# A tail rebuilt: last gh2 among the LayerNorm-backward rows, column sums by ones matmuls, the last modulation gradients on PE, two groups of products moved to GpSimd

## The chip, the cores and the metric

One core of one Trainium2 chip. The metric is the device time of one execution in microseconds (us), the median of several. On one core most runs of a kernel agree within 0.3%; every run quoted here is undisturbed. Engines are named as in the profile: PE (TensorE matmul), DVE (VectorE), ACT (ScalarE), POOL (GpSimd), SP (the queue that issues most DMAs).

## The reference

Forward and backward pass of a block with two LayerNorms, modulated by `c`: a spectral filter (rfft2, times a complex weight, irfft2) and a gated bilinear layer. Sequence 2048, width 576, hidden width 4608, bf16. Outputs: the forward result and the gradients of eight inputs.

```python
mod = (silu(c) @ w_mod).reshape(1, 6, 1, 576)          # sa, ca, ga, sb, cb, gb
h = layernorm(x) * (1 + ca) + sa
x = x + ga * irfft2(rfft2(h) * (w_r + 1j * w_i))       # spectral filter
h = layernorm(x) * (1 + cb) + sb
x = x + gb * (((h @ w_gate) * (h @ w_up)) @ w_down)    # gated bilinear
# ... vjp of all this for grad_out
```

## The kernel before

The change touches the last quarter of the kernel, after the last gate/up block. I cut that tail into four stages by events on PE: (1) the last gh2 (gradient that reaches the second LayerNorm) and its 16 LayerNorm-backward rows, with weight gradients as filler, up to the first inverse-stage matmul; (2) eight spectral units up to the first matmul of the final rows; (3) sixteen final rows up to the last column sum; (4) the end. "Filler" is a list of independent matmul blocks that the program deals out between dependent steps, so that PE has something to do. A list scheduler then orders the instructions of each engine by dependences and its own estimate of times; each engine runs its list in that order.

The complex multiply of a unit, and the loop of the units:

```python
def multiply(X, W, P1, P2, Y, SD, conj, u):
    tt(P1[:], X[:], W[:], MUL)                         # L457   tt = DVE tensor_tensor
    tt(P2[:], X[:], W[:, :, ::-1, :], MUL)             # L458
    tt(Y[:, 0], P1[:, :, 0, :], P1[:, :, 1, :], ADD)   # L459
    tt(Y[:, 1], P2[:, :, 1, :], P2[:, :, 0, :], SUB)   # L461
    if u:
        tt(SD[:, 0:2], Y[:, :, 0, :], Y[:, :, 1, :], ADD)   # L465
        tt(SD[:, 2:4], Y[:, :, 0, :], Y[:, :, 1, :], SUB)   # L466

load_X(0)                                              # ahead of the units
load_X(1)

def grad_W(u, gY):                                     # gradient of the spectral weights
    gw = gw_r.next()
    tt(Q[:], Xls[u][:], gY[:], MUL)                    # L1068
    tt(gw[:, :, 0, :], Q[:, :, 0, :], Q[:, :, 1, :], ADD)
    tt(Q[:], Xls[u][:], gY[:, :, ::-1, :], MUL)
    tt(gw[:, :, 1, :], Q[:, :, 0, :], Q[:, :, 1, :], SUB)
    # ... stores
for s in range(9):
    # ... stage_b of unit s (PE, ACT, DVE), filler
    if s:
        u = s - 1
        X = X_r.next()
        stage_c(u, Zs[u], X, RS)                       # PE L441, copy by ACT L442
        multiply(X, Ws[u], P1, P2, Y_t, SD_t, True, u)
        fill.run(4.0)
        stage_ci(u, Y_t, SD_t, Gt)                     # PE L492, needs the multiply
        gws[u] = grad_W(u, X)
        # ... loads of W and X for unit u + 2
```

The column sums of a row, and one final row:

```python
def diag_sums(a, b, j, b0, b1, c1, col):               # ten small matmuls
    for m, (d0, n) in enumerate(CH):
        mm(bank[0:n, b1, col + m:col + m + 1], a[:, d0:d0 + n], ones[:, 0:1], ...)
        # ... and a[:, block].T @ b[:, block], of which only the diagonal is used

ts(n[:], n[:], rstd1[:, jj:jj + 1], nmr1[:, jj:jj + 1], MUL, ADD)   # DVE
ln_bwd(gh, n, mod[:, SCA, :], ...)
fill.run(2.5)
diag_sums(gh, n, jj, 6, 7, 0, 64)
fill.run(2.5)
```

## Time and profile before

| stage, us (profiled run) | (1) | (2) | (3) | end | span |
|---|---|---|---|---|---|
| before | 113.3 | 106.1 | 109.8 | 34.4 | 1569.0 |

The median is 1572.26 us (1569.24 to 1573.04, 4 runs). The first matmul of the final rows is at 1424.8; the prediction put it at about 1428, so its second stage is 3.3 us longer and its third shorter.

```profile
PE bank L492 <- DVE arena L465: 3.7, 5, 1.4
```

### The profile page before, as it was taken

The page shows a single profiled execution, that of the slowest core. Times are in us where ns is not written, and L with a number is a line of the kernel's source. Part 1 is how long each engine was busy: PE and PEld are TensorE (multiplying, and loading weights), DVE is VectorE, ACT ScalarE, POOL GpSimd, SP SyncE. Part 2 cuts the span into 40 slices and gives each one's busy share as a digit, 9 for nine tenths or more (in the row PEclk, how much of TensorE's full clock was granted, in tenths as well). Part 3 has the DMA queues.
Part 4 walks back from the last instruction along what each step waited for, and adds up shares of the span by engine and source line. Part 5 has one row for each costly group of instructions (what it writes and reads, how often), then busy time and mean ns, then how long its engine had stood idle before and what let it go on. Part 6 is the DMA issues. An engine that isn't in the chain of part 4 may idle for free. (4 is left out here: it accounts for less than half of the span.)

```text
span 1569.0 us, 28400 instructions
## 1 busy us (share of the span) xinstructions
PE 1479.0 (94%) x11245; PEld 989.8 (63%) x11268; DVE 811.0 (52%) x1800; ACT 515.6 (33%) x1017; POOL 261.1 (17%) x380
## 2 busy tenths in 40 slices
PE   7799997999999999999999999999999888999991
PEld 4344442677677668667767766866776666676771
DVE  6424496633543453353354345335337765778865
ACT  5656665212212221221221122122123344344331
POOL 1122321212202202211220220221110110000000
PEclk9899999999999999999999999999999999999995
DMA  9655886977558557646755854765663597567941
GB/s 277 193 145 158 205 232 157 196 152 169 123 106 184 128 109 153 150 120 127 168 128 101 184 128 108 155 145 123 128 156 100 163 258 226 157 182 206 267 123 49
DMA packets 440998, 248.76 MB, mean 159 GB/s; under 512 B 318048, under 2 KB 418336, under 8 KB 440352
## 3 DMA queue, kind: packets, MB, share of 16 engines
q1 hardware_dynamic: 418256, 177.19, 50.4%
q0 software_dynamic: 22464, 69.62, 14.5%
q8 instruction: 88, 1.44, 0.4%
q14 instruction: 46, 0.38, 0.1%
q10 hardware_dynamic: 144, 0.13, 0.0%
HBM read 96.90 MB, written 74.20 MB: 109 GB/s over the span
## 5 line engine op out<-in xcount | busy, mean ns | idle before, releaser
L852 DVE TENSOR_TENSOR arena<-arena,bank 128x576 f32<-128x576 f32 x272 | 204.9, 754 | 305.1 <-PE bank L846 305.1
L740 ACT CAST arena<-bank 128x512 bf16<-128x512 f32 x144 | 84.4, 586 | 390.4 <-PE bank L730 373.4
L846 PE MATMUL bank<-arena 128*128 128x288 bf16 x576 | 164.6, 286 | 0.0
L843 PE MATMUL bank<-arena 128*128 128x288 bf16 x576 | 163.9, 285 | 0.5 <-DVE arena L850 0.2
L845 PE MATMUL bank<-arena 128*128 128x288 bf16 x576 | 164.3, 285 | 0.0
L844 PE MATMUL bank<-arena 128*128 128x288 bf16 x576 | 164.1, 285 | 0.0
L785 PE MATMUL bank<-arena 128*128 128x256 bf16 x1152 | 150.3, 274 | 7.9 <-ACT arena L790 5.4
L1032 PE MATMUL bank<-arena 128*128 128x288 bf16 x1152 | 152.9, 288 | 0.0
L765 PE MATMUL bank<-arena 128*128 128x288 bf16 x1152 | 147.9, 289 | 4.5 <-DVE arena L773 4.5
L734 PE MATMUL bank<-arena 128*128 128x512 bf16 x576 | 149.6, 382 | 1.5 <-DMA arena<-arena 1.5
L789 PE MATMUL bank<-arena 128*128 128x256 bf16 x1152 | 150.6, 274 | 0.0
L736 PE MATMUL bank<-arena 128*128 128x512 bf16 x576 | 148.7, 381 | 0.0
L765 PEld LDWEIGHTS <-arena 128*128 128x128 bf16 x1152 | 113.2, 99 | 37.4 <-issue 4.7
L1032 PEld LDWEIGHTS <-arena 128*128 128x128 bf16 x1152 | 111.0, 98 | 32.0 <-issue 3.2
L785 PEld LDWEIGHTS <-arena 128*128 128x128 bf16 x1152 | 111.3, 98 | 24.8 <-issue 11.4
L789 PEld LDWEIGHTS <-arena 128*128 128x128 bf16 x1152 | 112.5, 98 | 13.9
L744 DVE TENSOR_TENSOR arena<-arena 128x512 bf16<-128x512 bf16 x144 | 61.2, 425 | 107.1 <-ACT arena L740 107.1
L790 ACT CAST arena<-bank 128x256 bf16<-128x256 f32 x144 | 53.5, 372 | 184.9 <-PE bank L789 184.9
L734 PEld LDWEIGHTS <-arena 128*128 128x128 bf16 x576 | 50.4, 98 | 80.6 <-issue 31.6
L736 PEld LDWEIGHTS <-arena 128*128 128x128 bf16 x576 | 56.6, 98 | 68.6 <-issue 1.1
L741 ACT CAST arena<-bank 128x512 bf16<-128x512 f32 x144 | 84.8, 589 | 24.7 <-PE bank L736 23.3
L321 ACT CAST arena<-bank 128x1024 bf16<-128x1024 f32 x72 | 72.8, 1011 | 55.3 <-PE bank L317 27.9
(217 smaller groups left out, 2206.3 us busy)
## 6 DMA issues: line engine op xcount, KB each, us to landing
ghh_d<-arena POOLq DMA_DIRECT2D x72, 256.0 KB, 3.6
arena<-ghh_d POOLq DMA_DIRECT2D x36, 512.0 KB, 5.4
hh_d<-arena SPq DMA_DIRECT2D x36, 512.0 KB, 4.5
arena<-hh_d SPq DMA_DIRECT2D x16, 1152.0 KB, 7.7
out_dram<-arena POOLq DMA_DIRECT2D x36, 256.0 KB, 5.1
arena<-in_B_w_down_dram POOLq DMA_DIRECT2D x18, 288.0 KB, 4.1
out_dram<-arena POOLq DMA_DIRECT2D x36, 144.0 KB, 5.6
arena<-in_B_w_down_dram SPq DMA_DIRECT2D x4, 1296.0 KB, 8.4
```

The costliest lines, as they stand in the source:

```text
L734: mm(bank[:, bg, :], w[:, m, fs], h2T[:, js, m, :], odd == 0 and m == 0, odd == 1 and m == 3)
L736: mm(bank[:, bu, :], w[:, 4 + k, fs], h2T[:, js, m, :], odd == 0 and k == 0, odd == 1 and k == 3)
L741: ac.copy(u[:], bank[:, bu, :])
L765: mm(bank[:, b0 + h, 0:288], sf[:, 0, fb, j, :], go[:, j, 288 * h:288 * h + 288], j == 0, j == 15)
L785: mm(bank[:, st["b"], 0:256], h2p[:, j, 128 * m:128 * m + 128], sf[:, 1 + w, :, j, :], j == 0, False)
L789: mm(bank[:, st["b"], 0:256], h2p[:, j, 128 * m:128 * m + 128], sf[:, 1 + w, :, j, :], False, j == 15)
L843: mm(o, xT[:, 1, 0, cs], wT[p][:, 0, 0, hs], True, False)
L844: mm(o, xT[:, 2, 0, cs], wT[p][:, 0, 1, hs], False, False)
L845: mm(o, xT[:, 1, 1, cs], wT[p][:, 1, 0, hs], False, False)
L846: mm(o, xT[:, 2, 1, cs], wT[p][:, 1, 1, hs], False, True)
L852: tt(dst, dst, src, ADD)
L1032: mm(bank[:, yb, 0:288], hl[:, fb % 18, 128 * (j % 2):128 * (j % 2) + 128], wdr[:, fb, 288 * h:288 * h + 288], fb == 0, fb == 35)
```

## The change

Its intent: less PE work in the rows (column sums of whole rows by a matmul with ones on column groups, instead of diagonal blocks), less DVE work in the rows and the units (normalisation to ACT, three row products and the gradient of the spectral weights to POOL), gh2 spread among the rows instead of ahead of them, and no serial gradient work at the end: four of the six modulation gradients go into the units, the last two are made by small matmuls with a transposed `w_mod`. Buffers move with it, so the loads of X now start only after the last weight gradients. The core of the diff:

```diff
+        def column_sums(srcs, b, j, w):
+            for h in range(2):
+                for i, a in enumerate(srcs):
+                    mm(bank[w * i:w * i + w, b + h, 0:288], ones[:, 0:w], a[:, 288 * h:288 * h + 288], j == 0, j == 15, ...)
@@ rows of stage 1
-            ts(n[:], n[:], rstd2[:, j:j + 1], nmr2[:, j:j + 1], MUL, ADD)
+            act(n[:], n[:], ACT.Identity, bias=nmr2[:, j:j + 1], scale=rstd2[:, j:j + 1])
-            tt(gn[:], gx[:], mod[:, SGA, :], MUL)
-            fold(Fj.unsqueeze(1), gn.unsqueeze(1), 1)
-            diag_sums(b, n, j, 2, 3, 0, 192)
-            diag_sums(gx, yl[j], j, 5, 3, 64, None)
+            po.tensor_tensor(gs[:, 0:288], gx[:, 0:288], mod[:, SGA, 0:288], MUL)
+            po.tensor_tensor(gs[:, 288:576], gx[:, 575:287:-1], mod[:, SGA, 575:287:-1], MUL)
+            po.tensor_tensor(pg[:], gx[:], yl[j][:], MUL)
+            column_sums([acc_b(j), q, pg], 2, j, 32)      # two rows later
@@ spectral units
-        load_X(0)
-        load_X(1)
-            tt(Q[:], Xls[u][:], gY[:], MUL)
+            gt = po.tensor_tensor
+            gt(Q[:], Xls[u][:], gY[:], MUL)
             # ... the other three alike
+                if s == 1:
+                    fill.flush()                          # the last weight gradients
+                    fill = yfill
+                    load_X(0)
+                    load_X(1)
                 stage_ci(u, Y_t, SD_t, Gt)
                 gws[u] = grad_W(u, X)
+                if mgs:
+                    mod_grad(*mgs.pop(0))                 # six groups, one per unit
@@ final rows and end (cut)
-                ts(n[:], n[:], rstd1[:, jj:jj + 1], nmr1[:, jj:jj + 1], MUL, ADD)
+                act(n[:], n[:], ACT.Identity, bias=nmr1[:, jj:jj + 1], scale=rstd1[:, jj:jj + 1])
-                diag_sums(gh, n, jj, 6, 7, 0, 64)
+                column_sums([gh, q], 6, jj, 64)
+            if j == 2:
+                sp.dma_start_transpose(out=wmT[:], in_=w_mod[:, 0:2 * D])
+                # fold of the early modulation gradients: 4 small matmuls into bank 0, 2 DVE copies
-        mod_grad(SCA, mod[:, SCA, :])
-        mod_grad(SSA, mod[:, SSA, :])
+        # ... ten one-row matmuls, nine scaled rows, 45 one-column matmuls with wmT
```

## The prediction

> **What bounds the kernel now.** I read the page's parts 1 and 2 first: PE is busy 94% of the span, so the 366 us after the last gate/up block (1203 us on) is the only place with room. Then I cut the tail, from the end of the last gate/up matmuls (1205.2, from PE's timeline), at the first inverse-stage matmul (1318.6), the first of the final rows (about 1428) and the last column sum (1534.7), and asked for the busy time of each engine in each stretch. Columns: window, length, then busy us (and count) of PE, PEld, DVE, ACT, POOL, then granted clock, DMA share, GB/s.
>
> ```profile
> 1205.20:1318.60 113.40, 97.49 (x921) 75.64 (x920) 82.08 (x211) 52.32 (x127) 13.63 (x20) 0.94 0.84 227
> 1318.60:1428.00 109.40, 102.72 (x817) 73.82 (x817) 73.62 (x114) 40.79 (x95) 0.00 (x0) 0.97 0.62 169
> 1428.00:1534.70 106.70, 104.67 (x921) 79.28 (x919) 83.12 (x236) 43.06 (x110) 0.00 (x0) 1.00 0.68 193
> 1534.70:1569.00 34.30, 1.63 (x6) 0.40 (x4) 16.44 (x53) 2.48 (x8) 0.00 (x0) 0.54 0.17 49
> ```
>
> The reader should see four different stages. The first (last gh2, LayerNorm-backward rows with the last weight gradients as filler) leaves PE idle for 16 us; the second (eight spectral units) and third (sixteen final rows) are PE-bound through the filler, the y products; the last has almost no PE and 34 us of serial work. Its length is mostly one store. In the DMA view (out<-in, queue, count, KB each, us to landing) that is the last line, issued at 1552.5 and landing 15.2 us later:
>
> ```profile
> out_dram<-arena SPq DMA_DIRECT2D x1, 1.1 KB, 15.2
> ```
>
> The chain of waits of a spectral unit, from the timeline, is the next thing to keep in mind: PE's unit matmuls (L441), ACT's copy (L442), DVE's complex multiply (L457 to L466) and back to PE (L492), with four filler blocks of nine matmuls (L1032) laid over it.
>
> ```profile
> 1354.44 1.15 PE L441 MATMUL bank<-arena 128*128 128x290 bf16 x8
> 1355.18 1.21 ACT L442 ACTIVATE arena<-bank 128x580 bf16<-128x580 f32 x2
> 1356.41 0.76 DVE L457 TENSOR_TENSOR arena<-arena 128x1160 bf16<-128x1160 bf16 x1 [3.54 <-ACT arena L442]
> ...
> 1358.51 1.36 DVE L1068 TENSOR_TENSOR arena<-arena 128x1160 f32<-128x1160 bf16 x1
> 1359.79 0.45 DVE L465 TENSOR_TENSOR arena<-arena 128x580 bf16<-128x580 bf16 x1
> 1360.16 0.45 DVE L466 TENSOR_TENSOR arena<-arena 128x580 bf16<-128x580 bf16 x1
> 1360.30 0.28 PE L492 MATMUL bank<-arena 128*128 128x256 bf16 x1 [1.40 <-DVE arena L465]
> ```
>
> X is ready at 1356.4 and PE goes on at 1360.3: 3.9 us, just about hidden by the filler. Units follow every 12.7 us. L1068 to L1071 are the gradient of the spectral weights, 1.36 + 0.76 + 1.37 + 0.76 = 4.2 us of DVE per unit.
>
> **What the Trainium skill says.** (1) "SBUF — State Buffer", section "Who interferes with whom": a DVE instruction with two SBUF inputs contends with a GpSimd instruction that reads SBUF; whoever starts first holds the shared port for the whole instruction. The trace agrees. Of 36 POOL additions two met such a DVE instruction, and both times it took 1.7 us where its median is 0.45:
>
> ```profile
> 1235.91 1.41 POOL L774 TENSOR_TENSOR arena<-arena 128x576 f32<-128x576 f32 x1
> 1235.96 1.69 DVE L906 TENSOR_TENSOR arena<-arena 128x576 bf16<-128x576 bf16 x1
> ```
>
> ```profile
> 1285.68 1.42 POOL L774 TENSOR_TENSOR arena<-arena 128x576 f32<-128x576 f32 x1
> 1285.74 1.68 DVE L908 TENSOR_TENSOR arena<-arena 128x576 bf16<-128x576 bf16 x1
> ```
>
> A third POOL addition (1156.42) overlapped a DVE instruction with one PSUM input; that took its usual 0.76. (2) "GPSIMD Engine Reference", section "Elementwise — side-by-side cycle accounting": about 2.6 cycles per element for a two-input operation. The trace gives 1413 ns for 576 columns; with some 0.2 us fixed (an estimate) that is 2.1 ns per column, so 0.8 us for 288, 2.6 for 1160, 1.4 for 580. (3) "TensorE: Matmul & The Clock Gate", section "Part 3: Packing small matmuls": matmuls on different column groups run concurrently. The trace agrees: the two 32-column matmuls L947 and L948 start at the same time, 1230.72.
>
> **The change, part by part.**
>
> First stage. Removed on PE: per row 15 diagonal-sum matmuls (1.07 us from first start to the next block, 1228.34 to 1229.41) and 6 of stage a (0.48 us), 16 rows: 24.8 us. Added: per row six 288-column sums on three column groups, two packs of 0.13, four matmuls of 256 columns (0.11 each) and half of eight packed 128-column ones (0.12): 0.82 us, 13 us in all. Some 9 us of filler is kept for the next stage. PE work falls from 97.5 to about 75 us, and gh2 (16.4 us, so far ahead of the rows) now lies among them. DVE loses per row the normalisation (0.43), one scale (0.36), the SGA product (0.45) and the fold (0.60); it gains split gh2 additions. ACT gets more: per row two scale-and-bias passes at 0.87 (L668's form), two accumulating passes at 0.88, two evacuations at 0.38 and a remainder: 4.5 us, 72 us for sixteen, 78 with the gradients' evacuations. So ACT, not PE, is the floor. With first and last row's latency 85 us instead of 113: -28. POOL gets 0.8 + 0.8 + 1.4 = 3.0 us per row.
>
> Second stage. The y filler starts one unit later (51 us of credit here instead of 62) but 9 us of gradients replace it: about -2.5. At the start the W loads stand behind two loads of 1.2 MB and the modulation weights; I allow 3.5 us of waiting. grad_W leaves DVE for POOL (2 x 2.6 + 2 x 1.4 = 8.0 us per unit), and the early modulation gradients enter DVE (18 pairs of 0.75 + 0.08 + 0.28: 20 us over eight units). If POOL disturbs nobody: +1 in all.
>
> Third stage. Ten sum matmuls per row (0.65) become two packs (0.26): 16 x 0.39 = -6.2; slightly more y filler (80 instead of 78 us): +1.7. Together -4.5. DVE loses the 30 us of modulation gradients, but it is not the bound.
>
> End. 15 us of modulation gradients on DVE go; in their place: copy 0.6, filler 4.4, ten small matmuls 0.8, copies 0.5, filler 4.4, 45 one-column matmuls some 3, four small DVE operations 0.6, issue 0.4, and again a store of 576 two-byte elements, 15.2: 30 us instead of 34.3, with 10 us of filler inside (already counted above as moved): -4.3.
>
> Sum without any disturbance: -28 + 1 - 4.5 - 4.3 = -36, so 1572 - 36 = 1536 us.
>
> **The rivals.** (a) The port lock. The new grad_W needs X and its load, so POOL becomes ready at the moment at which DVE's multiply does. Both then want the port, and the trace shows POOL getting in between two DVE instructions that stand back to back (L936 and L908 at 1285.7). If each of POOL's four operations comes between two of the six of DVE, the multiply takes 2.9 + about 7.5 = 10.4 us instead of 3.9, PE waits 6.5 us in every unit that is so hit, seven of eight: +45. In the rows the same lock costs DVE up to 2.5 us of each row; with DVE's own 3.6 us and ACT's 4.5 I take 5.8 us per row, so the first stage needs 100 instead of 85. Then the total is -13 + 46 - 4.5 - 4.3 = +24: 1596 us. For it: the two blocked instructions. Against it: only two are seen, and late X loads could let POOL run a unit behind, beside DVE work that is not on the path. (b) DMA. The first stage moved 227 GB/s at a share of 0.84, and DVE waited 9.9 us for row loads; the change preloads two instead of five of the y operands there, which helps, but a 2.7 MB load in front of the last rows' loads may delay row 15 by some 7 us: 1543. (c) The whole gain hidden: the end is still a serial chain behind a 15 us store, and rows gain only what ACT leaves: about 1555.
>
> **Range and chances.** I give the undisturbed sum, with (b)'s delay, a little over half and (a) a little under half: about 1562 us. A partial lock, which I hold likeliest, lies there too. Range 1520 (everything overlaps, the rows run at ACT's pace from the start) to 1604 (full lock). Faster by over 2% means below 1541: 0.36. Slower by over 2% means above 1604, the full lock with cold PE clock in the gaps: 0.18. Within: 0.46.
>
> **What would show it.** Right: the first stage shorter by 13 to 28 us, the third by 4 to 5, the end near 30 with a store that still takes 15 us to land; packs of three sums starting together. For (a): two-SBUF-input DVE operations of the multiply with means of 1.5 us and more instead of 0.45 to 0.76, PE waiting for the last of them before the inverse matmuls, units every 19 us, and a lower granted clock there. Against (a): units every 12.5 us and unchanged DVE means. The prediction is wrong at its root if the y filler runs dry, if a scheduled DVE instruction ahead of a multiply waits for a load, or if POOL needs far more or less than 2.1 ns per column.

## More of the kernel before

The prediction shows the stage table and one unit. For the argument two more readings count. The first is the DVE groups by shape in the second stage (source line, engine, operation, output<-input with shapes, count | busy us, mean ns | idle time before them): the steps of the multiply at their undisturbed durations. The second is PE's waits there (the waiting instruction, what released it: us in total, times, longest): PE waits 3.7 us for the multiply in all eight units.

```profile
L457 DVE TENSOR_TENSOR arena<-arena 128x1160 bf16<-128x1160 bf16 x8 | 6.1, 762 | 15.4 <-ACT arena L442 12.8 <-issue 2.2 <-DMA out_dram<-arena 0.3
L458 DVE TENSOR_TENSOR arena<-arena 128x1160 bf16<-128x1160 bf16 x8 | 6.0, 756 | 0.0
L459 DVE TENSOR_TENSOR arena<-arena 128x580 bf16<-128x580 bf16 x8 | 3.6, 455 | 0.0
```

In the changed kernel the multiply is L472 to L481 (L457 to L466 before), `grad_W` L1190 to L1193, PE's use of the multiply L507.

## The result and the profile after

The changed kernel takes 1626.72 us (median of 4 runs, 1626.04 to 1628.49), the kernel before 1572.26 in the same rounds: a ratio of 1.0352, interval 1.0334 to 1.037. Ratios here are the mean time of one kernel's fast runs over that of the other's of the same rounds, so not quite the ratio of the medians. The change is slower, outside the predicted range.

| stage, us | (1) | (2) | (3) | end | span |
|---|---|---|---|---|---|
| before | 113.3 | 106.1 | 109.8 | 34.4 | 1569.0 |
| changed | 103.2 | 168.4 | 117.7 | 28.5 | 1625.2 |
| difference | -10.1 | +62.3 | +7.9 | -5.9 | +56.2 |

The remaining 2.0 us arise before the tail. The busy time of each engine by stage, columns as in the prediction's table (window, length, busy us and count of PE, PEld, DVE, ACT, POOL, granted clock, DMA share, GB/s):

```profile
1207.20:1310.50 103.30, 82.67 (x729) 57.12 (x727) 84.23 (x167) 64.18 (x150) 57.75 (x64) 0.92 0.79 216
1310.50:1479.00 168.50, 118.83 (x799) 79.37 (x799) 104.70 (x126) 43.07 (x96) 66.65 (x36) 0.81 0.54 138
1479.00:1596.70 117.70, 109.73 (x856) 76.86 (x854) 62.84 (x162) 70.45 (x145) 0.00 (x0) 0.97 0.61 162
1596.70:1625.20 28.50, 11.31 (x132) 8.77 (x131) 5.14 (x20) 4.55 (x8) 0.00 (x0) 0.76 0.22 63
```

The loss is in the second stage. POOL is busy there for 67 us, and DVE got busier (104.7 us) although 34 us of work left it and some 20 came. No engine is at its bound: PE is idle for 50 us, and its granted clock is down to 0.81. The DVE groups of the stage, the same steps as before:

```profile
L473 DVE TENSOR_TENSOR arena<-arena 128x1160 bf16<-128x1160 bf16 x8 | 17.8, 2228 | 0.0
L476 DVE TENSOR_TENSOR arena<-arena 128x580 bf16<-128x580 bf16 x8 | 14.4, 1805 | 0.0
L474 DVE TENSOR_TENSOR arena<-arena 128x580 bf16<-128x580 bf16 x8 | 13.7, 1718 | 0.0
L480 DVE TENSOR_TENSOR arena<-arena 128x580 bf16<-128x580 bf16 x7 | 7.6, 1089 | 0.2
```

Shapes and types are unchanged, and the means went from some 455 (580 columns) and 756 ns (1160) to 1.1 to 2.2 us. One unit in the timeline (start, duration, instruction, in brackets the idle time before it and what ended that; lines of other work are left out) shows how:

```profile
1366.48 4.57 PE L1010 MATMUL bank<-arena 128*128 128x288 bf16 x36
1367.52 2.84 POOL L1190 TENSOR_TENSOR arena<-arena 128x1160 f32<-128x1160 bf16 x1 [11.10 <-DMA arena<-x_d]
1368.04 2.94 DVE L472 TENSOR_TENSOR arena<-arena 128x1160 bf16<-128x1160 bf16 x1
1370.43 1.61 POOL L1191 TENSOR_TENSOR arena<-arena 128x580 bf16<-128x580 f32 x1
1370.90 1.77 DVE L473 TENSOR_TENSOR arena<-arena 128x1160 bf16<-128x1160 bf16 x1
1372.12 2.56 POOL L1192 TENSOR_TENSOR arena<-arena 128x1160 f32<-128x1160 bf16 x1
1372.59 2.40 DVE L474 TENSOR_TENSOR arena<-arena 128x580 bf16<-128x580 bf16 x1
1374.75 1.31 POOL L1193 TENSOR_TENSOR arena<-arena 128x580 bf16<-128x580 f32 x1
1374.91 1.47 DVE L476 TENSOR_TENSOR arena<-arena 128x580 bf16<-128x580 bf16 x1
...
1377.09 0.39 PE L507 MATMUL bank<-arena 128*128 128x256 bf16 x1 [6.03 <-DVE arena L480]
...
1379.61 2.34 PE L1010 MATMUL bank<-arena 128*128 128x288 bf16 x9
```

The two engines take turns. Each DVE record begins 0.2 to 0.5 us after a POOL record and ends 0.3 to 0.6 us after that one's end, somewhat less than the DVE step takes undisturbed; by then the next POOL instruction is on record and in front again. The multiply runs from 1368.0 to 1377.4, 9.4 us instead of 2.9, and PE, whose filler of 36 matmuls is over at 1371.1, waits 6.0 us. Then the last line: nine filler matmuls take 2.34 us. In undisturbed units the same nine take 1.28 us. The Trainium skill ("TensorE: Matmul & The Clock Gate", section "Part 1: The HAM clock gate") says that the array falls to half rate after an idle window of some 3.4 us; this trace agrees: 6.0 us of idleness are followed by 1.8 times the duration, and the granted clock is 0.50 from 1377 to 1382 where it was 0.99 from 1362 to 1371. Over the stage, PE's waits for the multiply:

```profile
PE bank L507 <- DVE arena L480: 45.6, 7, 12.0
```

That is 45.6 us where it was 3.7. In four other units DVE's first step (L472) began 0.1 us ahead of POOL and kept its 0.76 us, but the steps behind it were held up all the same, and those multiplies took 9.1 to 9.5 us. Sorting the stage's DVE records by whether POOL was inside an addition or product as they began gives a rule without an exception for the multiply's 580-column steps: L474, L476, L480 and L481 took 1.28 to 2.63 us in the 19 cases inside and 0.45 to 0.46 in the 11 others.

### The profile page after: what moved, and what is told of

The parts are those of the page before. It is cut to its first block, busy times and chain, and to the rows that moved or that the text cites. A ratio compares the mean times of both kernels' runs of the same rounds, so it can differ in the third digit from the quotient of the medians.

```text
span 1625.2 us, 28183 instructions
## 1 busy us (share of the span) xinstructions
PE 1496.4 (92%) x11096; PEld 983.7 (61%) x11119; DVE 811.2 (50%) x1659; ACT 561.3 (35%) x1081; POOL 375.1 (23%) x465
## 4 chain that ended last, share of the span: by engine, by line
PE 76%; DVE 11%; DMA 4%; ACT 3%; SPq 2%; issue 2%; POOL 0%; DVEq 0%; ACTq 0%; POOLq 0%
PE bank L750 8%; PE bank L781 8%; PE bank L752 7%; PE bank L828 7%; PE bank L832 7%; PE bank L1010 5%; PE bank L887 4%; PE bank L890 4%; PE bank L889 4%; PE bank L888 4%; PE bank L324 3%; PE bank L328 3%; PE bank L745 2%; PE bank L848 2%; DMA arena<-in_B_w_down_dram 1%
## 5 line engine op out<-in xcount | busy, mean ns | idle before, releaser
L901 DVE TENSOR_TENSOR arena<-arena,bank 128x576 f32<-128x576 f32 x256 | 192.9, 754 | 305.2 <-PE bank L890 305.2
L887 PE MATMUL bank<-arena 128*128 128x288 bf16 x576 | 164.3, 285 | 2.9 <-ACT arena L833 2.0
L890 PE MATMUL bank<-arena 128*128 128x288 bf16 x576 | 164.9, 286 | 0.0
L889 PE MATMUL bank<-arena 128*128 128x288 bf16 x576 | 164.7, 286 | 0.0
L888 PE MATMUL bank<-arena 128*128 128x288 bf16 x576 | 164.4, 285 | 0.0
L1010 PE MATMUL bank<-arena 128*128 128x288 bf16 x1152 | 160.3, 296 | 0.0
L1010 PEld LDWEIGHTS <-arena 128*128 128x128 bf16 x1152 | 113.6, 101 | 39.1 <-issue 7.7
L781 PE MATMUL bank<-arena 128*128 128x288 bf16 x1024 | 128.1, 286 | 0.0
L828 PEld LDWEIGHTS <-arena 128*128 128x128 bf16 x1152 | 111.6, 98 | 18.4 <-issue 5.0
L832 PEld LDWEIGHTS <-arena 128*128 128x128 bf16 x1152 | 112.3, 98 | 14.3 <-issue 1.2
L781 PEld LDWEIGHTS <-arena 128*128 128x128 bf16 x1024 | 100.2, 98 | 28.2
L678 POOL DMA_DIRECT2D arena<-ghh_d x36 | 19.8, 551 | 394.8 <-DVE arena L759 364.5
L750 PEld LDWEIGHTS <-arena 128*128 128x128 bf16 x576 | 50.5, 98 | 80.0 <-issue 31.8
L752 PEld LDWEIGHTS <-arena 128*128 128x128 bf16 x576 | 56.6, 98 | 68.6 <-issue 1.1
```

Source lines behind the costliest of these rows:

```text
L750: mm(bank[:, bg, :], w[:, m, fs], h2T[:, js, m, :], odd == 0 and m == 0, odd == 1 and m == 3)
L752: mm(bank[:, bu, :], w[:, 4 + k, fs], h2T[:, js, m, :], odd == 0 and k == 0, odd == 1 and k == 3)
L781: mm(bank[:, b0 + h, 0:288], sf[:, 0, fb, j, :], go[:, j, 288 * h:288 * h + 288], j == 0, j == 15)
L828: mm(bank[:, st["b"], 0:256], h2p[:, j, 128 * m:128 * m + 128], sf[:, 1 + w, :, j, :], j == 0, False)
L832: mm(bank[:, st["b"], 0:256], h2p[:, j, 128 * m:128 * m + 128], sf[:, 1 + w, :, j, :], False, j == 15)
L887: mm(o, xT[:, 1, 0, cs], wT[p][:, 0, 0, hs], True, False)
```

## The experiments

Seventeen kernels ran, in six sets on their chips, each timed in three rounds against the kernel before (its medians in these sets: 1567 to 1571 us). All results were correct but for one. Three of the edits (e3, e12, e14) did not bring about the order that they were made for, and so tested nothing. A unit's time is the distance from its first matmul to the next unit's.

| label | time, us | ratio to before | (1) | (2) | (3) | end |
|---|---|---|---|---|---|---|
| e1_gradw_on_dve | 1577.72 | 1.0047 | 103.2 | 122.6 | 113.7 | 28.6 |
| e2_rows_on_dve | 1610.47 | 1.0261 | 89.2 | 165.4 | 116.2 | 28.4 |
| e3_gradw_after_multiply | 1624.05 | 1.0350 | 103.3 | 163.7 | 118.8 | 27.6 |
| e4_before_gradw_on_pool | 1625.93 | 1.0358 | 113.5 | 160.5 | 109.1 | 35.6 |
| e5_gradw_behind_multiply | 1593.82 | 1.0163 | 103.1 | 135.6 | 116.9 | 27.3 |
| e6_pool_writes_only | 1575.06 | 1.0043 | 103.0 | 118.2 | 118.2 | 28.3 |
| e7_both_on_dve | 1563.06 | 0.9966 | 90.5 | 122.3 | 113.2 | 27.5 |
| e8_and_norm_on_dve | 1565.60 | 0.9985 | 88.8 | 123.2 | 116.8 | 26.7 |
| e9_sums_a_row_later | 1560.05 | 0.9952 | 89.4 | 122.7 | 109.8 | 27.7 |
| e10_modgrads_in_rows | 1555.57 | 0.9923 | 89.1 | 112.2 | 115.8 | 27.9 |
| e12_transpose_late | 1562.03 | 0.9958 | 89.2 | 123.3 | 113.0 | 28.2 |
| e11_all_repairs | 1557.28 | 0.9937 | 89.2 | 114.2 | 116.2 | 27.9 |
| e13_fold_at_end | 1548.99 | 0.9879 | 88.9 | 112.5 | 110.0 | 28.8 |
| e14_gradw_a_unit_later | 1557.51 | 0.9932 | 89.3 | 114.6 | 115.8 | 27.6 |
| e15_first_gradw_forced_later | 1550.32 | 0.9882 | 89.3 | 117.3 | 110.0 | 28.7 |
| e17_only_pieces_held | 1554.19 | 0.9896 | 89.1 | 117.3 | 111.0 | 29.5 |
| e16_no_load_before_multiply | 1547.37 | 0.9855 | 89.7 | 107.8 | 110.6 | 29.5 |

### First question: is it POOL's reading beside DVE?

**The gradient back on DVE.**

```diff
-            gt = po.tensor_tensor
+            gt = ve.tensor_tensor
```

> The changed kernel with one edit: the four operations of the spectral-weight gradient are back on DVE. Theory A (port lock between POOL's two-input operations and DVE's multiply): spectral units go from about 20 us back to 13 to 14, the second stage from 168.5 to 113 to 120 us, the time to 1570 to 1580 us. Rival B (the stage is long because of the modulation gradients put on DVE, or loads queued late): DVE gets 4.2 us more per unit, so the time stays at 1620 us or grows. Rival C (cold clock alone, whatever caused the first gap): in between, about 1605 us.

Measured: 1577.72 us, 49 us less than the changed kernel; the second stage is 45.8 us shorter, though at 122.6 still above the 113 to 120 expected (mostly the third unit, 21.2 us; see the third question). Its row of the stage table, to be held against the changed kernel's second line:

```profile
1311.50:1434.10 122.60, 104.07 (x799) 73.16 (x799) 86.67 (x158) 42.84 (x96) 1.73 (x4) 0.92 0.72 187
```

The same 799 PE records take 104.1 busy us instead of 118.8. So of the 45.8 us, 14.8 are the same matmuls running at a lower clock and the other 31 are idle time. Moving 34 us of work back onto DVE made DVE 18 us less busy.

**The three row products back on DVE.**

```diff
-            po.tensor_tensor(gs[:, 0:288], gx[:, 0:288], mod[:, SGA, 0:288], MUL)
+            ve.tensor_tensor(gs[:, 0:288], gx[:, 0:288], mod[:, SGA, 0:288], MUL)
             # ... the other two alike
```

> The changed kernel with the three POOL multiplies of each LayerNorm-backward row on DVE instead. Theory A: DVE's two-input operations there lose their waits (means of 0.74 us back to 0.45) but DVE gets about 1.0 us of own work per row, so the first stage goes from 103 to 92 to 100 us: time 1615 to 1625 us. Rival B (the rows are set by ACT's chain and by loads): first stage within 2 us of 103, time within 3 us of 1627. Rival D (POOL really relieved DVE): first stage longer by 5 us or more, 1632 us or more.

Measured: 1610.47 us, 16 us less, better than the 1615 to 1625 expected; the first stage falls from 103.2 to 89.2. The DVE group of the one-input scaling in these rows, first of the changed kernel, then of this run:

```profile
L956 DVE TENSOR_SCALAR arena<-arena 128x576 bf16<-128x576 bf16 x16 | 11.7, 735 | 0.0
```

```profile
L956 DVE TENSOR_SCALAR arena<-arena 128x576 bf16<-128x576 bf16 x16 | 5.8, 366 | 0.0
```

An instruction with a single SBUF input is held up too. The Trainium skill ("SBUF — State Buffer", section "Who interferes with whom") lists `tensor_scalar` among the operations that can take the shared ports in a two-port mode; the trace agrees. The prediction had only counted two-input ones.

**The gradient on POOL in the kernel before,** the four operations of `grad_W` as `po.tensor_tensor`, nothing else.

> The kernel before with the four grad_W operations moved to POOL and nothing else. Theory A: the multiply is split by POOL's operations, units of 19 to 20 us instead of 12.7, time 1572 + 45 to 60 = 1617 to 1632 us. Rival B (the modulation gradients and the order of loads in the changed kernel do it): within 10 us of 1572, or faster, because DVE loses 34 us of work.

Measured: 1625.93 us. This one edit costs 56 us by itself, 54 of them in the second stage (160.5 after 106.1), where PE's wait for the multiply rises from 3.7 to 38.9 us. So the lock needs nothing else of the change. That the sum equals the change's own loss is chance: there, gains and other losses of some 16 us cancel.

**The gradient kept on POOL, but behind the multiply.** The first attempt failed as an experiment:

```diff
+            po.tensor_copy(small[:, 110:111], SD_t[:, 3, 0:1] if u else Y_t[:, 1, 1, 0:1])
             gt = po.tensor_tensor
```

> The changed kernel with grad_W still on POOL, but behind a one-column POOL copy that reads the last result of DVE's multiply, so that POOL starts when the multiply is over. Theory A: the multiply takes 3 us again; POOL's 8 us fit beside PE-bound work, units of 13 to 15 us, time 1575 to 1595 us; what remains is POOL meeting the modulation gradients on DVE. Rival E (POOL is simply too slow, and its late stores hold up the queue of loads): starting POOL later makes it worse, 1627 us or more.

Measured: 1624.05 us, no change. The trace shows why: nothing made the gradient depend on the tiny copy, so the scheduler put the copy behind the gradient, and POOL started beside the multiply as before. The run says nothing for or against either theory. Mended, the copy writes into Q, which the gradient overwrites:

```diff
+            po.tensor_copy(Q[:, 0, 0, 0:1], SD_t[:, 3, 0:1] if u else Y_t[:, 1, 1, 0:1])
             gt = po.tensor_tensor
```

> The changed kernel with one tiny POOL copy ahead of each unit's gradient. It reads the last value of the multiply and writes into Q, so that this time the order is forced by the data: the same 8 us of POOL work in each unit, but none of it beside that unit's multiply. Theory A (the port lock on the multiply): the multiply is back to 3.9 us, units of 13 to 15 us, second stage 120 to 135 instead of 168 us, total 1577 to 1593. Rival B (the cost comes from POOL being slow as such: late gradients, late stores, late reversals by PE, buffers freed late): POOL ends 4 us later than before, so units of 20 us or more, total 1627 or more.

Measured: 1593.82 us, 33 us less with the same work on the same engine, just outside what I expected (1577 to 1593). In six of the eight multiplies every step is back to 0.45 or 0.76 us; the second and the last still meet the gradient of the unit before (they take 7.0 and 6.0 us), which is why L472 and L473 have means of 1.0 us. The fifth unit takes 17.0 us (12.6 with the gradient on DVE), but not through POOL: DVE waits 4.9 us for modulation weights ahead of its multiply. When POOL works is thus worth 33 of the 49 us that moving the gradient off POOL brings.

**POOL equally long, but writing only** (outputs 2 and 3 wrong on purpose):

```diff
-            gt = po.tensor_tensor
-            gt(Q[:], Xls[u][:], gY[:], MUL)
-            # ... and the other three
+            po.tensor_tensor(Q[:, 0, 0, 0:1], Xls[u][:, 0, 0, 0:1], gY[:, 0, 0, 0:1], MUL)
+            for _ in range(7):
+                po.memset(Q[:], 0.0)
+            po.tensor_copy(gw[:, 0, 0, 0:1], Q[:, 0, 0, 0:1])
+            po.memset(gw[:], 0.0)
```

> The changed kernel with POOL's four gradient operations replaced by seven memsets of Q, one of gw and two operations of one column (outputs 2 and 3 wrong on purpose), some 9 us of POOL that hardly reads, ready at the same moment and with the same stores and reversals behind it. Theory A, if the lock needs a POOL operation that reads: DVE's six operations keep 0.45 to 0.76 us, units of about 12.7 us, second stage 110 to 125, total about 1570 to 1580. If any POOL access to SBUF blocks: means of 1.5 us or more, units of about 20. Rival B: units of 20 us whatever POOL does.

Measured: 1575.06 us, 52 us less, although POOL is busy for 69 us of the second stage, as long as in the changed kernel. The DVE and POOL groups of that stage, and one unit:

```profile
L473 DVE TENSOR_TENSOR arena<-arena 128x1160 bf16<-128x1160 bf16 x8 | 6.0, 752 | 0.0
L476 DVE TENSOR_TENSOR arena<-arena 128x580 bf16<-128x580 bf16 x8 | 3.6, 451 | 0.0
L1160 DVE TENSOR_SCALAR arena<-arena 128x576 bf16<-128x576 bf16 x18 | 12.0, 666 | 0.5
```

```profile
L1191 POOL MEMSET arena<- 128x1160 f32 x56 | 60.0, 1072 | 3.2
```

```profile
1367.76 7.80 POOL L1191 MEMSET arena<- 128x1160 f32 x7
1368.01 0.76 DVE L472 TENSOR_TENSOR arena<-arena 128x1160 bf16<-128x1160 bf16 x1 [1.27 <-ACT arena L457]
```

All of the multiply lies inside POOL's memsets and keeps its duration to 0.02 us. So it is POOL's reading that holds up a DVE operation with two SBUF inputs; late gradients or late stores (rival B) would have stayed. The third group line is the exception, and the same page foresees it, saying that the two-port modes contend with GpSimd in general: the scaling L1160 has a mean of 666 ns here, up to 1.29 us, where it takes 0.37 us alone.

**Both back on DVE** (the first two edits together).

> The changed kernel with both the gradient and the three row products on DVE, POOL empty in the whole tail (the first two experiments together). Theory A, effects add: 1626.7 - 49 - 16 = about 1562, ratio 0.993 to 0.997 to the kernel before: second stage 122, first 89. If both hide behind a common floor (the loads): 1570 or more.

Measured: 1563.06 us, as the sum said (1562). The change without its POOL part is 0.3% faster than before; the undisturbed sum had promised 2.3%. The rest asks where the difference went: this run's stages are 90.5, 122.3, 113.2 and 27.5, against 85, 107, 105 and 30 by the prediction's terms, from the same cuts.

### Second question: the third stage

PE's waits in the third stage of the changed kernel:

```profile
PE bank L524 <- DVE arena L1298: 3.9, 1, 3.9
PE bank L964 <- DVE arena L949: 2.3, 5, 0.8
PE bank L964 <- ACT arena L1280: 1.7, 3, 0.8
```

PE's column sums (L964) wait for DVE and ACT of the same row, and once a row's first matmul (L524) waits for L1298, a copy of the fold of the early modulation gradients out of bank 0. The trace leads this longest wait further back (queue of SP, then ACT and DVE, other lines left out):

```profile
1486.00 7.24 SPq L1291 DMA_TRANSPOSE arena<-in_w_mod_dram  x1
1496.90 0.87 ACT L1282 ACTIVATE arena<-arena 128x576 bf16<-128x576 bf16 x1 [2.94 <-DMA arena<-in_A_x_dram]
1498.56 0.46 DVE L957 TENSOR_TENSOR arena<-arena 128x576 bf16<-128x576 bf16 x1 [3.62 <-ACT arena L955]
```

The transposing load holds SP's queue for 7.24 us, and the load of an x row is issued behind it, at 1493.95. ACT's normalisation (L1282) waits for that row, L955 stands behind it on ACT, DVE's L957 waits for L955, and the copy L1298 (1499.54) stands behind L957. I had suspected both links from L964 alone, the normalisation that moved to ACT and the transposing load, and tried each on the run with both on DVE. There, however, the wait for the fold is only 0.4 us, so neither run could remove it.

```diff
-                act(n[:], n[:], ACT.Identity, bias=nmr1[:, jj:jj + 1], scale=rstd1[:, jj:jj + 1])
+                ts(n[:], n[:], rstd1[:, jj:jj + 1], nmr1[:, jj:jj + 1], MUL, ADD)
```

> As the run with both on DVE, and the final rows' normalisation back from ACT to DVE. Theory C (ACT, in order, waits for the x row at the normalisation and holds up the copy of gh behind it, so column sums and PE wait): the third stage falls from about 114 to 108 or less, total 4 to 7 us under that run. Rival D (the transposing load of the modulation weights that holds the queue for 7 us alone lengthens the stage): no change within 2 us.

Measured: 1565.60 us, 2.5 us more than the run with both on DVE, the third stage 116.8: the gain that theory C promised is not there. The wait for the fold is back at 2.7 us; again an x row's load stands behind the transposing load (1428.17 to 1434.60), and DVE, now with the normalisation, waits 2.2 us for it ahead of the copy. The next edit moves the transposing load from the third iteration of the rows to the last, in the program:

```diff
-            if j == 2:
+            if j == 15:
                 sp.dma_start_transpose(out=wmT[:], in_=w_mod[:, 0:2 * D])
+            if j == 2:
                 # fold as before
```

> As the run with both on DVE, but the transposing load of the modulation weights moves from the third iteration of the final rows to the last, behind all row loads. Rival D (it holds the queue for 7 us and starves the rows): third stage 109 to 111, total 1559 to 1561, the end not longer. If the other waits of the stage count alone: no change within 2 us, or a longer end if the small matmuls now wait for it.

Measured: 1562.03 us, the third stage 113.0 after 113.2. But the load did not move: the trace has it at 1427.58, 7.9 us after the stage's start (8.0 without the edit). Nothing held it back, and the scheduler pulled it forward again. So the run says nothing about rival D, which stays untested; in every later run with this edit, too, the load is issued 7 to 14 us after the stage's start. What did help is to let PE find the sums ready:

```diff
-                column_sums([gh, q], 6, jj, 64)
+                if jj:
+                    column_sums(prev, 6, jj - 1, 64)
+                prev = [gh, q]
```

> As the run with both on DVE (third stage 113.2 us), but each final row's column sums are issued one row later, so that PE finds them ready. Theory E (the two packs cost what they should, but stand right behind the row's DVE and ACT work and PE, in order, waits 5 us for them and then pays slower filler): the third stage falls to 105 to 108, total 1556 to 1560. Rival F (the packs themselves are as slow as the ten small matmuls were, so nothing was to be gained): third stage 112 to 114, total unchanged within 2 us.

Measured: 1560.05 us, the third stage 109.8, 3.4 us less but short of the 105 to 108 expected. PE's timeline, summed from each start to the next start, gives the cost of the sums: 9.4 us before, 9.1 in the changed kernel, 10.4 in the run with both on DVE, 5.2 here. The packs cost little; standing right behind the row's DVE work, they paid the saving back as waiting. Theory E holds in kind, with half its size. (The edit also gives `gh` and `q`, which now live a row longer, a third buffer each; whether that alone helps was not tried.)

### Third question: the second stage, and a better version

First, the modulation gradients, cut into 18 pieces and put among the final rows in the program, with their first loads after the W loads:

```diff
-                if mgs:
-                    mod_grad(*mgs.pop(0))
+                if s in (5, 6):
+                    load_wm2(mgs[s - 5][0], mgs[s - 5][2])
@@ final rows
+            for _ in range(0 if j == 0 or not pieces else 2 if j < 6 else 1):
+                mod_piece(*pieces.pop(0))
+            if j == 14:                                   # was j == 2
                 # fold
```

> As the run with both on DVE (second stage 122.3 us), but the six modulation-gradient groups leave the spectral units: cut into 18 pieces they go among the final rows, and their first two loads are issued in units five and six instead of ahead of the W loads. Theory G (the second stage is 12 us over my 110 because DVE, in order, waits for the modulation weights ahead of a multiply and has 13 us of work per unit, and because the W loads stand behind those of the modulation weights): second stage 108 to 112, units of 12 to 13 us, the third stage at most 4 us longer, total 1552 to 1559. Rival H (the second stage is long because 9 us of weight gradients were moved into it and nothing else): second stage 119 or more, total 1563 or more.

Measured: 1555.57 us, second stage 112.2 as expected, but not as I had argued: the trace has all 18 pieces still within the units, where the scheduler pulled them into DVE's gaps. What changed is that the W loads no longer stand behind those of the modulation weights (second unit 11.2 us instead of 16.5) and that the pieces are more finely placed (sixth unit 12.6 instead of 15.8). The third unit stays at 21.0, PE waiting once for 6.9 us. All three repairs together (of which the transposing load, as said, did not take effect):

> The three repairs together (sums a row later, modulation gradients among the final rows, transposing load last) on the kernel with POOL empty. If each theory holds and the effects add: first stage 90, second 110, third 106 to 110, end 28: 1543 to 1552, a ratio to the kernel before of 0.983 to 0.988. If the rows' DVE becomes the bound with the gradients in it (3.9 + 1.2 us per row of 6.6, so it should not): third stage 115 or more and about 1556.

Measured: 1557.28 us, not the 1543 to 1552 expected: they did not add up. The third stage is 116.2 instead of 109.8, and PE's longest wait there is the fold again, which now stands in the second-last row:

```profile
PE bank L524 <- DVE arena L1303: 4.1, 1, 4.1
```

So the fold was moved behind the rows, into the filler of the end:

```diff
-            if j == 14:
-                tt(fold_f[:], ident[:, 0:64], ident[:, 64:128], ADD)
-                # ... four small matmuls, two copies
         ac.copy(halves(R2), bank[:, 6:8, 0:288])
-        fill.run(4.0)
+        fill.run(2.0)
+        # fold
+        fill.run(2.0)
```

> As the run with all three repairs, but the fold of the early modulation gradients (four small matmuls and two DVE copies out of bank 0, which PE needs for the next row) moves from among the final rows into the filler of the end. Theory I (the row after the fold waits for DVE's copy, 4.1 us in that run's trace, and that is what its third stage of 116.2 has over the 109.8 of the run with only the sums a row later): third stage 109 to 112, end at most 1 us longer, total 1549 to 1554. Rival J (the gradient pieces on DVE lengthen the rows): third stage 114 or more, total within 2 us of that run.

Measured: 1548.99 us, the third stage 110.0, the end 28.8: theory I holds. The second stage now is the one with most to gain, by its third unit of 21 us. There DVE, in order, waits for the first X load with unit one's gradient, ahead of unit two's multiply. A first attempt to move the gradient:

```diff
+                Xh[u] = X
+                if u:
+                    gws[u - 1] = grad_W(u - 1, Xh[u - 1])   # one unit later
```

> As the run with the fold at the end, but each unit's gradient is issued one unit later, behind the next unit's multiply, on DVE. Theory K (the third unit of 21 us is the first X load, which the change moved from before the units to after the last weight gradients: DVE, in order, waits 3.8 us for it with the gradient of unit one ahead of the multiply of unit two): third unit 12 to 14 us, second stage 105 to 109 instead of 114, total 1541 to 1547. Rival L (the third unit is long for another reason, such as its W load or filler): it stays at 19 or more and the total does not move by more than 2 us.

Measured: 1557.51 us, third unit 19.3. This run failed as a test of theory K: DVE's order still has the first gradient (1321.97) ahead of that multiply (1326.25), presumably since the scheduler believed X to be there; the later reversals of the gradients cost PE 6 us in the third stage. With the order forced for the first unit alone, through Q as above:

```diff
+                if u == 1:
+                    ve.tensor_copy(Q[:, 0, 0, 0:1], SD_t[:, 3, 0:1])
+                    gws[0] = grad_W(0, X0)
```

> As the run with the fold at the end, but the gradient of the first unit alone is issued behind the second unit's multiply, its order forced this time by a tiny copy that reads that multiply's last value and writes into Q; the two gradients then follow one another. Theory K (DVE, in order, waits 4.2 us for the first X load with unit one's gradient ahead of unit two's multiply, so PE waits 7 us): third unit 13 to 16 us instead of 21.4, second stage 106 to 109 instead of 112.5, total 1543 to 1546. If the 8 us of gradients behind it only push the delay into the next unit (fourth unit 17 or more): total 1547 to 1551. Rival L: third unit 19 or more.

Measured: 1550.32 us, third unit 20.0 and fourth 17.0: by the letter of what I expected, rival L, with some delay pushed on as well. The trace names the reason (DVE, third unit):

```profile
1325.62 0.76 DVE L1159 SCALAR_TENSOR_TENSOR arena<-arena 128x576 bf16<-128x576 bf16 x1 [8.07 <-DMA arena<-in_w_mod_dram]
...
1326.31 0.76 DVE L472 TENSOR_TENSOR arena<-arena 128x1160 bf16<-128x1160 bf16 x1
```

Now it is a piece of the modulation gradients that waits for its load, 8.1 us, right ahead of the multiply. To complete the square, the pieces were held back by a clearing of their accumulators that depends on the third multiply, once with the first gradient forced later and once without:

```diff
-        ve.memset(gsc, 0.0)
@@ unit 2, behind the multiply
+                    ts(small[:, 50:68], SD_t[:, 3, 0:18], 0.0, None, MUL)
```

> As the run with the fold at the end, the modulation-gradient pieces held back alone, the first unit's gradient ahead of the second multiply as it was. Theory M: DVE still waits some 4 us for the first X load and then does 4.2 us of gradient ahead of the multiply; third unit 18 to 20 us, a total within 3 us of that run (1549). If the pieces were the cause alone: third unit 14 or less, total 1543 or less.

> As the run with the first gradient forced later, and the modulation-gradient pieces too are held back, by a tiny operation that clears their accumulators from a value of the third unit's multiply (times zero). Ahead of the second unit's multiply there is then no DVE instruction that waits for a load. Theory M (the wait is passed on from load to load: whichever load-bound instruction the order puts ahead of that multiply holds it up): third unit 12 to 14 us, fourth at most 17, second stage 106 to 111 instead of 117, total 1541 to 1547. Against M: third unit 19 or more.

Measured: with the pieces held alone 1554.19 us and a third unit of 23.0, both more than theory M said (within 3 us of 1549, and 18 to 20), DVE waiting 6.5 us for X:

```profile
1324.08 1.37 DVE L1188 TENSOR_TENSOR arena<-arena 128x1160 f32<-128x1160 bf16 x1 [6.49 <-DMA arena<-X_d]
```

With neither load ahead of the multiply: 1547.37 us, third unit 12.4, second stage 107.8. Either load alone keeps the unit at 20 us or more; only taking both away frees it. (The profiled runs with one load alone, 1554.69 and 1556.82 us, are the slowest of their four, so their stages are on the long side; 20 and 23 against 12.4 us are not in doubt.) The Trainium skill ("PSUM — Partial Sum Buffer", section "Engine vs sequencer instructions") calls the VectorE queue strict first in, first out, and these two traces agree: DVE idles 8.1 and 6.5 us for a load, and the multiply behind, whose X ACT had finished at 1320.8 in both, begins at 1326.3 and 1328.4. This last version has a ratio of 0.9855 (0.9838 to 0.9871) to the kernel before: 1.5% faster, and it beats both kernels.

## Why the prediction was wrong

**The step that failed** is the weighting: "I give the undisturbed sum, with (b)'s delay, a little over half and (a) a little under half", and "a partial lock, which I hold likeliest". The lock was full. (Nor does 1562 follow from these weights: 1543 at a little over half and 1596 at a little under half give about 1568.) The reason given against it, "late X loads could let POOL run a unit behind", did not come true: POOL did wait for its X loads at first, but then started in the same stretch as the multiply, in seven of eight units. The two blocked additions shown in the kernel before were enough to know the price of one meeting; that both engines become ready at the same event, the arrival of X, made the meeting the normal case and should have settled the odds. All the signs that the prediction names for (a) appeared: means of 1.1 to 2.2 us, PE's waits, units of mostly 17 to 21 us, and a clock of 0.81.

**The lock's size in the units** looks right in the waiting, 45 us predicted as 6.5 in each of seven units and 45.6 measured, but that is partly luck. With the gradient on DVE PE still waits 13.2 us for the multiply, so the lock's own share is some 32; alone in the kernel before it adds 35. And one part of the price was missing from the sum. By the run with the gradient on DVE the lock cost 45.8 us in this stage, 31 of them idleness and 14.8 a colder clock on the same matmuls. The prediction named a cold clock only as a way beyond its upper end and did not price it.

**The second missing term** is the order of loads in DVE's queue, for which the prediction allowed 3.5 us. (Its own terms, 51 instead of 62 us of filler and 9 of gradients, make -2, not -2.5.) From the run with both on DVE to the last version the second stage falls by 14.5 us (122.3 to 107.8): modulation weights and the first X load, which the change issues later, are kept out of the way of the W loads and of the second unit's multiply; finer pieces, three of which leave the stage, have a part in it that was not measured alone. The +62.3 us are then 45.8 for the lock, 14.5 for this, 1.7 by which 107.8 exceeds the 106.1 of before, and 0.3 between the two runs on DVE. The "+1" for a POOL that disturbs nobody was about right for a version that has neither trouble.

**First stage.** Predicted -28 undisturbed and -13 with the lock; measured -24.1 (row products on DVE, 89.2) and -10.1. The mechanism and both sizes hold within 4 us, and the packs of three sums do start together (1233.00 in the trace). That also the one-input scaling is held up was not foreseen.

**Third stage.** Predicted -4.5, measured +7.9. The term "two packs (0.26): 16 x 0.39 = -6.2" was mis-sized twice: free of waits the sums fell from 9.4 to 5.2 us, 4.2 less, and as built they fell by only 0.3, because they wait for the row's own DVE and ACT work. The wait for the fold's copy in bank 0 (3.9 us, and 1.9 more on the 16 filler matmuls behind it, at 240 ns each instead of 123) was not in the sum. In the trace it comes from an x row loaded behind the transposing load; that is read from the trace and not shown by a run, since no run moved that load. Even with the sums later and the fold moved the stage is 110.0, equal to before. In the run with the sums a row later, PE's timeline charges 4.2 us less to the sums, but 2.0 more to the filler, 1.3 more to the row's own matmuls and 0.8 to the fold, which adds up to nothing. The filler's matmuls are not slower there (123 ns from start to start in both kernels); nearly all of the 2.0 us lie at the ends of its blocks, before PE goes on with the row (7.1 us over 31 such places instead of 5.2 over 32), which points to PE waiting for the row there.

**The end.** Predicted -4.3, measured -5.9, and the tiny store still takes 14.9 us to land (15.2 before). Right.

**The rival's total** of 1596 us was thus 31 us short of the measured 1627: some 16 in the second stage (62.3 against 46), 12 in the third (7.9 against -4.5), 3 in the first, 2 before the tail, and 2 back at the end. The true time lay outside a range whose top assumed just that total and a little more.

## What to carry to other kernels

Before moving DVE work to GpSimd, ask which event makes both engines ready: if it is the same one, and both read two operands from SBUF, they take turns, as they did here, and the work moved comes back on the critical path. Price a wait of PE at its length plus the slower matmuls behind it (here 31 and 14.8 us). On in-order queues an instruction that depends on a load belongs behind the instructions that others wait for, and if a scheduler decides the order, only a data dependence holds it there; check the order in the trace before believing an experiment (three of seventeen here had not changed it).

## What the Trainium skill lacked or had wrong

- "SBUF — State Buffer", section "Who interferes with whom": right on every point tried (reads against two-input operations, memsets harmless to them at 0.45 and 0.76 us, `tensor_scalar` held up, 366 to 735 ns). It lacks what happens with back-to-back instructions on both engines: they alternate, and six DVE steps of 2.9 us together with four POOL steps took 9.4 us.
- The same section gives the lock to whoever issues first. It does not say that POOL can be in front at every turn, as in the unit shown, where each of its four operations began 0.2 to 0.5 us ahead of the DVE step that it held up.
- "TensorE: Matmul & The Clock Gate", section "Part 1: The HAM clock gate": it puts the warm-up ramp at under 1% of a typical span, and the same section, further down, prices gaps that recur. Gaps of some 6 us, once per unit, made the same matmuls 14.8 us longer, a third of what the lock cost in the second stage. The first figure alone, though 14.8 us are just 0.9% of 1625, would mislead.
- "DMA: Bandwidth & Descriptors", section "DMA Transpose (X-bar)": it gives no issue time for a transposing load of this size on its queue. Here it was 7.24 us in the changed kernel for 576 by 1152 elements (6.5 in the run with both on DVE).
